# A written-out order replaced by another: loads ahead, no zero matmuls in the head, the last bank read after its last matmul

## The chip, the cores and the metric

The kernel runs on one core of one Trainium2 chip. The metric is the time of one execution on the device in microseconds. Runs before: 199.13, 199.85 and 200.0 us, median 199.85.

## The reference

Attention with a local window and a few global keys, then a two-matrix network with a squared ReLU:

```python
batch, n_heads, seq, head_dim = (4, 8, 768, 64)
n_global, n_local = (8, 96)
...
scores = scale * np.matmul(q, k.transpose(0, 1, 3, 2))
...
keep = is_global | is_local
...
scores = np.where(keep, scores + bias, -1000000000.0)   # bias = -slope of the head * distance
a = softmax(scores);  x = np.matmul(a, v)               # x: 3072 tokens x 512
h = x @ w_in                                            # 512 x 2048
r = np.maximum(h, 0.0)
g = r * r
return (g @ w_out).astype(np.float32)                   # 2048 x 512
```

(The lines of the mask and the softmax are drawn together.) Inputs and output are float32.

## The kernel before, in words

The 3072 tokens are 24 tiles of 128 rows, 6 to each batch element; two tiles make a block, 12 in all. Tile j goes through these steps, which the kernel registers one by one (`plan.op`) under short names:

- `ld` / `load`: POOL starts DMAs that bring q, k and v of the tile to SBUF as bf16 (L304 to L312, issued at L307 for the first loads and at L310 later). Tile 0 is an exception: its q and k come in float32 by SP's queue (L319) into `plain`.
- `tr` (L502): TensorE transposes q (`tr.0.j`) or k (`tr.1.j`) into a PSUM bank, `T` copies the bank to `qkT` on DVE or ACT (L517). From tile 8 on one DMA transpose on SP's queue does both (L536).
- `bias` (tiles 0 to 2, L572) and `sc` (L590): score matmuls into banks, this tile's keys and the tile's before. `gk`, `gv` (L723, L795) copy the eight global keys and values into the neighbour tile; `gv` runs on POOL, DVE or ACT.
- `exp` (L661, on ACT), `mul` (L683, times the exponentiated mask, on DVE), `pv` (L739, values), `norm` (L773, reciprocal and product on DVE).
- `trx` and `xT` (L812 to L833): x transposed on TensorE for tiles 0 to 7, by a DMA on SP's queue for the others (L837).

Blocks 0 and 1 multiply plainly by w_in, in 8 steps (`s1`, L1054, with `relu` L1082 and `sq` L1094), block 0 by w_out in 8 steps (`s2`, L1334). Blocks 2 to 11 take their products in seven parts by sums and differences of quarter matrices: `xs` (L909), `h` (L943) with copies `u` (L973), `c` (L991), `q` (L1011) for w_in, `sum` (L1163), `s2` (L1206), `part` (L1248) and `o` (L1280) for w_out; `isum` and `wsum` prepare the weights. `st` stores the output on SP's queue (L1306).

What sets the order: nothing is scheduled when the kernel is built. `ORDER` (L57) is a string of step names in the order in which the steps are emitted; `Plan.run` (L39) walks through it. A word such as `bias.0.0:23` is step bias of tile 0 in PSUM banks 2 and 3, `T.1.0@V` is step T on DVE (`@A` ACT, `@P` POOL), `s1.0.3#2` is the second step of that name. Each engine runs its own instructions in the order of the string and waits on semaphores for what it reads and for the buffer that it writes; POOL and SP are queues of their own in the same way. The `deps`, `key` and costs that the steps are registered with do not act on a given order.

In the head, after eight warm-up matmuls on a zeroed tile (L371), the string has the transpose of q of tile 0, then the step `warm`: eight more matmuls on zeros (L530, `NKEEP`), then the transpose of k of tile 0. In the last block the half bank of part `p3` is filled in two cuts, of 192 and 64 columns (L1201); the string ends

```
... s2.11.p3.0 s2.11.p3.1
s2.11.p3.0#2 o.11.p3 s2.11.p3.1#2 st.11.0#2 o.11.p3#2 st.11.0#3
```

so the first cut is read by DVE (`o.11.p3`) between the two halves of the second cut.

The loads' order of registration (L414) is not their order of issue; that is in the string too. Its first words issue win.3.0 (a piece of w_in), k of tile 1, q of tile 1, v of tile 0, and loads stay mixed with the work, with `gv.2@P`, `gv.3@P` and `gv.4@P` between them on POOL.

Of the kernel before, what the change touches and what calls it, by code (L numbers as in the profile page):

```python
# [67 lines left out]
pv.4.0:2 ld.wout.1 sq.0.2@V sc.5.0:4157 ld.wout.0 s1.0.4:6 relu.1.2@A exp.5.1.1 s1.0.1:3 sq.1.3@A exp.5.0.0 relu.0.4@V
s1.1.4:7 ld.wout.2 norm.4.0 pv.4.1:4 gv.4@P norm.4.1 sq.0.4@A load.7 exp.5.1.0 sq.1.2@A relu.1.4@A s1.0.0:6 gate.9
ld.wout.4 mul.5.0 s1.0.0#2 sq.1.4@A s1.0.0#3 s1.1.5:2 trx.4:1 exp.5.0.1 relu.1.6@V s1.1.1:4 ld.wout.5 s1.0.1#2  # L70
relu.1.1@A E0.1 mul.5.1 relu.1.5@A pv.5.0:7 s1.1.7:0 s1.1.0:5 sq.1.1@V norm.5.0 ld.wout.6 E0.0 sq.1.5@V tr.1.6:4
sq.1.6@A pv.5.1:2 relu.1.7@A tr.0.6:7 s1.0.0#4 norm.5.1 xT.4@A sq.1.7@A h.2.0.p2:0 ld.wout.7 T.1.6@V h.2.1.p2:1
trx.5:2 xT.5@V relu.1.0@A sq.1.0@A gate.14 h.2.0.p1:5 xs.2.0 s1.0.5:4 sum.1.2 s1.0.7:2 relu.0.1@A xs.2.1 gate.10
sum.1.0 sum.1.1 relu.0.0@A T.0.6@A sc.6.0:36 wsum.0.0 sum.1.3 sq.0.0@A sq.0.1@A s2.0.0.0:7 relu.0.7@A s2.0.1.0 load.9
exp.6.0.0 xs.2.2 s2.0.2.0 exp.6.1.0 s2.0.3.0 s2.0.0.1:2 s2.0.1.1 wsum.2.0 relu.0.5@A sq.0.7@A s2.0.2.1 load.8 mul.6.0
wsum.1.0 s2.0.3.1 tr.0.7:3 tr.1.7:6 gate.15 isum.0.0 h.2.1.p1:4 T.0.7@A s2.0.4.0 isum.0.1 s2.1.p1.0:3 isum.3.1 T.1.7@A
sq.0.5@A pv.6.0:6 isum.1.1 s2.0.4.1 s2.0.5.1 u.2.0.1@A c.2.0.c11 s2.0.5.0 gate.11 u.2.1.1@A h.2.1.p6 q.2.0.c11@A
isum.1.0 T.8 s2.0.6.1 u.2.1.2@A s2.0.6.0 isum.3.0 pv.6.1:0 h.2.0.p6 wsum.2.1 wsum.0.1 s2.1.p1.1 s2.0.7.1 c.2.1.c11
norm.6.0 gate.13 o.0.1@V st.0.1 s2.0.7.0 h.2.1.p7 part.1.p1@A s2.1.p6.0 u.2.0.2@A o.0.0@A u.2.1.3@A h.2.0.p7 h.2.1.p4
T.9 norm.6.1 wsum.3.0 u.2.0.3@A sc.7.0:1762 c.2.1.c21@A wsum.1.1 h.2.1.p5:0 c.2.1.c22 q.2.1.c11@A s2.1.p2.0:4  # L80
exp.7.1.0 exp.7.0.0 isum.2.1 load.10 h.2.0.p4 exp.7.0.1 mul.7.0 exp.7.1.1 s2.1.p2.1 isum.2.0 s2.2.p1.0:7 q.2.1.c21@A
mul.7.1 h.2.0.p5:1 s2.1.p6.1 part.1.p6@A trx.6:6 gate.12 c.2.0.c21@A load.12 pv.7.0:2 xT.6@A c.2.0.c22 q.2.1.c22@A
q.2.0.c22@A s2.2.p1.1 h.2.1.p3 s2.1.p7.0 wsum.3.1 o.1.p2 norm.7.0 h.2.0.p3 pv.7.1:5 s2.1.p7.1 q.2.0.c21@A st.0.0
c.2.1.c12 s2.1.p5.0 s2.1.p5.1 part.1.p7@A q.2.1.c12@A s2.1.p4.0 T.10 s2.1.p4.1 c.2.0.c12 gk.7@V q.2.0.c12@A o.1.p5
o.1.p4@A sc.8.0:6201 st.1.1 part.2.p1@A s2.1.p3.0 norm.7.1 sum.2.0 sum.2.1 s2.1.p3.1 trx.7:5 xT.7@V o.1.p3 h.3.0.p1:3
exp.8.1.0 gk.8@V h.3.1.p1:2 exp.8.0.0 exp.8.1.1 exp.8.0.1 h.3.0.p2:6 xs.3.0 u.3.1.1@A sc.9.0:1540 s2.2.p6.0 mul.8.0
xs.3.1 mul.8.1 u.3.0.1@A h.3.0.p6 exp.9.0.1 exp.9.1.1 gv.7@V h.3.1.p2:4 c.3.0.c11 h.3.1.p6 c.3.1.c11 exp.9.0.0
pv.8.0:0 s2.2.p6.1 pv.8.1:6 load.11 norm.8.0 u.3.1.2@A s2.2.p2.0:1 sum.2.2 gv.8@P q.3.1.c11@A norm.8.1 xT.8 h.3.1.p7
h.3.0.p5:4 u.3.0.2@A h.3.0.p7 s2.2.p2.1 exp.9.1.0 st.1.0 part.2.p6@A xs.3.2 u.3.1.3@A q.3.0.c11@A h.3.1.p5:0 s2.2.p7.0
u.3.0.3@A mul.9.1 mul.9.0 s2.2.p7.1 c.3.1.c22 T.12 c.3.0.c22 pv.9.0:6 h.3.1.p3 o.2.p2 h.3.0.p4 c.3.1.c12 load.15  # L90
norm.9.0 q.3.1.c22@A h.3.0.p3 s2.3.p1.0:5 s2.3.p1.1 c.3.0.c12 q.3.0.c22@A pv.9.1:0 c.3.0.c21@A part.2.p7@A norm.9.1
q.3.1.c12@A h.3.1.p4 q.3.0.c12@A h.4.0.p1:3 c.3.1.c21@A s2.2.p5.0 part.3.p1@A gk.9@V sc.10.0:6402 s2.2.p5.1
q.3.0.c21@A sum.3.0 sum.3.1 s2.2.p4.0 s2.2.p4.1 exp.10.1.0 sum.2.3 exp.10.0.0 exp.10.0.1 h.4.0.p2:4 T.11 u.4.0.1@A
exp.10.1.1 gk.10@V gv.9@A s2.3.p6.0 o.2.p5 mul.10.0 c.4.0.c11 xT.9 h.4.1.p1:6 o.2.p4@A mul.10.1 s2.2.p3.0 s2.2.p3.1
q.3.1.c21@A s2.3.p2.0:0 sum.3.2 u.4.1.1@A pv.10.0:2 pv.10.1:4 s2.3.p6.1 xs.4.0 gate.17 o.2.p3 part.3.p6@A xs.4.1
s2.3.p2.1 norm.10.0 h.4.0.p6 h.4.1.p6 q.4.0.c11@A gv.10@A norm.10.1 u.4.0.2@A load.13 s2.3.p7.0 sc.11.0:7124 u.4.1.2@A
sum.3.3 h.4.0.p7 h.4.1.p7 xs.4.2 exp.11.1.0 o.3.p2 exp.11.0.0 u.4.0.3@V s2.3.p7.1 sc.12.0:17 exp.11.1.1 exp.11.0.1
gate.16 xT.10 h.4.0.p4 c.4.0.c21@A mul.11.0 st.2.0 mul.11.1 h.4.1.p2:4 c.4.1.c11 exp.12.1.0 s2.3.p5.0 pv.11.0:2
pv.11.1:3 s2.3.p5.1 norm.11.0 part.3.p7@A h.4.0.p5:7 q.4.1.c11@A u.4.1.3@A norm.11.1 h.4.1.p5:4 q.4.0.c21@A gate.20
s2.3.p4.0 c.4.0.c22 load.14 s2.3.p4.1 h.4.0.p3 T.13 gate.18 load.16 c.4.1.c22 exp.12.0.0 h.4.1.p4 q.4.1.c22@A h.4.1.p3  # L100
xT.11 s2.4.p2.0:2 h.5.0.p1:3 q.4.0.c22@A o.3.p5 mul.12.0 c.4.0.c12 o.3.p4@A c.4.1.c21@A u.5.0.1@A c.4.1.c12 T.15
s2.3.p3.0 q.4.0.c12@A s2.3.p3.1 q.4.1.c12@V q.4.1.c21@A h.5.0.p2:1 o.3.p3 sc.13.0:5764 st.3.1 st.2.1 h.5.1.p1:0
exp.13.0.0 T.14 s2.4.p2.1 c.5.0.c11 exp.13.1.0 pv.12.1:1 q.5.0.c11@A s2.4.p1.0:5 xs.5.0 sum.4.0 pv.12.0:7 xs.5.1
s2.4.p1.1 mul.13.0 h.5.0.p6 gk.13@V u.5.1.1@A exp.13.0.1 h.5.1.p6 exp.13.1.1 h.5.0.p5:6 sum.4.1 norm.12.0 norm.12.1
h.5.1.p2:4 xs.5.2 mul.13.1 c.5.1.c11 h.5.1.p5:7 u.5.1.2@A sum.4.2 gate.19 part.4.p1@A h.5.1.p7 u.5.0.2@A h.5.0.p7
o.4.p2 u.5.0.3@A c.5.0.c22 pv.13.0:1 u.5.1.3@A norm.13.0 s2.4.p6.0 s2.4.p6.1 xT.12 st.3.0 q.5.1.c11@A T.16 part.4.p6@A
h.5.0.p4 pv.13.1:4 s2.4.p5.0 sum.4.3 c.5.0.c21@A h.5.0.p3 h.5.1.p4 q.5.0.c22@A s2.4.p7.0 norm.13.1 s2.4.p7.1 s2.4.p5.1
c.5.0.c12 q.5.0.c21@A kl.15@V part.4.p7@A c.5.1.c22 q.5.0.c12@A sc.14.0:1346 o.4.p5 s2.4.p4.0 xT.13 exp.14.0.1 kl.14@V
h.5.1.p3 gv.13@P q.5.1.c22@V c.5.1.c12 c.5.1.c21@A s2.4.p4.1 load.17 h.6.0.p1:4 s2.4.p3.0 s2.4.p3.1 exp.14.1.1
exp.14.1.0 exp.14.0.0 sc.15.0:0673 mul.14.1 mul.14.0 xs.6.0 o.4.p4@A xs.6.1 h.6.0.p2:1 o.4.p3 q.5.1.c12@A s2.5.p1.0:5  # L110
u.6.0.1@A c.6.0.c11 exp.15.0.0 exp.15.1.0 exp.15.1.1 sum.5.0 s2.5.p1.1 h.6.0.p6 u.6.0.2@A exp.15.0.1 sum.5.1 load.18
h.6.0.p5:2 part.5.p1@A pv.14.0:0 norm.14.0 pv.14.1:6 h.6.1.p1:1 u.6.1.1@A h.6.0.p7 gv.14@P st.4.0 s2.5.p6.0 u.6.0.3@A
# [1319 lines left out]
```

## Time and profile before

| | |
|---|---|
| runs, median (lowest to highest) | 199.85 us (199.13 to 200.0) |
| profiled execution: its time | 199.37 us |
| its span on the core | 197.6 us |
| granted TensorE clock | 1.00 |
| HBM read / written | 27.26 MB / 6.29 MB |
| output DMAs of 256 KB, issue to landing | 2.5 us |

The span is the time from the first instruction to the last; the execution's own time has 1.8 us around it. PE is TensorE's matmuls, PEld its weight loads, DVE VectorE, ACT ScalarE, POOL GpSimd, SP SyncE; SPq is the queue of DMAs that SP issues. Busy times are unions of the spans of instructions, and neighbours on one engine overlap by some 0.1 us, so that a queue of instructions moves faster than the sum of their durations. A line of the waits reads: engine, what it was to write, its line, then for what it waited: us in total, times, longest. A line of the chain reads: start, length, what held the end at that time. L numbers are lines of the kernel before.

### The profile page before, as it was taken

How to read it: one execution, taken by the hardware profiler on the slowest of the kernel's cores; microseconds unless marked ns; L12 is line 12 of the kernel's file. 1: busy time of each engine (PE TensorE's matmuls, PEld its weight loads, DVE VectorE, ACT ScalarE, POOL GpSimd, SP SyncE). 2: the span in 40 equal slices, each digit the busy share in tenths (PEclk: the TensorE clock that was granted, in tenths of full speed). 3: DMA queues.
4: the chain of work that ended last, by engine and by line, in shares of the span. 5: the costliest groups of instructions: out<-in, count | busy, mean ns of one | idle time of the engine just before them, and what ended most of it. 6: DMA issues, size and time to landing. Idle time of an engine off the chain costs nothing.

```text
span 197.6 us, 6777 instructions
## 1 busy us (share of the span) xinstructions
PE 191.9 (97%) x2776; PEld 169.6 (86%) x2776; DVE 173.2 (88%) x423; ACT 163.0 (82%) x335; POOL 80.4 (41%) x101
## 2 busy tenths in 40 slices
...
PEclk9999999999999999999999999999999999999999
...
GB/s 127 153 158 171 181 181 185 182 202 159 139 209 191 75 200 88 145 174 210 151 129 203 114 124 194 160 121 92 136 81 116 154 55 56 27 30 163 0 106 106
DMA packets 111857, 26.91 MB, mean 136 GB/s; under 512 B 103379, under 2 KB 109011, under 8 KB 111827
## 3 DMA queue, kind: packets, MB, share of 16 engines
...
HBM read 27.26 MB, written 6.29 MB: 170 GB/s over the span
## 4 chain that ended last, share of the span: by engine, by line
PE 95%; DVE 2%; issue 1%; ACT 0%; DVEq 0%
PE bank L1212 35%; PE bank L950 32%; PE bank L1061 7%; PE bank L599 6%; PE bank L748 5%; PE bank L1339 4%; PE bank L372 2%; PE bank L506 2%; PE bank L532 1%; DVE qkT L433 1%; PE bank L816 1%; PE bank L579 0%; ACT qkT L429 0%; DVE o L1287 0%; DVE v L433 0%
## 5 line engine op out<-in xcount | busy, mean ns | idle before, releaser
L1015 ACT ACTIVATE hs<-hr 128x512 bf16<-128x512 f32 x72 | 44.8, 641 | 5.1 <-DVE hr L995 4.7
L665 ACT ACTIVATE esc<-bank 128x512 bf16<-128x512 f32 x78 | 42.9, 614 | 1.3 <-PE bank L599 1.0
L1212 PE MATMUL bank<-wsum,hsum 128*128 128x256 bf16 x264 | 36.2, 273 | 0.0
L1212 PEld LDWEIGHTS <-hsum 128*128 128x128 bf16 x360 | 32.1, 98 | 4.1 <-issue 0.5
L995 DVE CUSTOM_DVE_ANT_0 hr<-bank,early 128x512 f32<-128x512 f32 x45 | 30.4, 685 | 2.5 <-PE bank L950 1.5
L950 PEld LDWEIGHTS <-win 128*128 128x128 bf16 x480 | 29.7, 98 | 1.0
L950 PEld LDWEIGHTS <-qk_first 128*128 128x128 bf16 x480 | 29.7, 98 | 1.0
L429 ACT COPY early<-bank 128x512 f32<-128x512 f32 x42 | 24.5, 591 | 3.6 <-PE bank L950 3.3
L690 DVE TENSOR_TENSOR at<-esc,E 128x1024 bf16<-128x1024 bf16 x39 | 26.7, 696 | 0.1
L1212 PEld LDWEIGHTS <-hs 128*128 128x128 bf16 x264 | 24.0, 98 | 2.6
L310 POOL DMA_DIRECT2D qk<-in_q_dram x18 | 16.0, 890 | 21.9 <-DMA qkT<-qk 20.6
L1212 PE MATMUL bank<-wout,hs 128*128 128x256 bf16 x176 | 24.9, 273 | 0.0
L310 POOL DMA_DIRECT2D v<-in_v_dram x18 | 16.0, 888 | 18.3 <-DVE v L480 14.9
L950 PE MATMUL bank<-xT,win 128*128 128x128 bf16 x320 | 23.4, 219 | 0.0
L431 POOL COPY v<-v 8x520 bf16<-8x520 bf16 x8 | 5.7, 718 | 43.3 <-PE bank L748 43.3
L950 PE MATMUL bank<-xs,qk_first 128*128 128x128 bf16 x320 | 22.8, 219 | 0.0
L779 DVE TENSOR_TENSOR x<-bank,rs 128x256 bf16<-128x256 f32 x48 | 20.4, 425 | 1.7
L865 ACT ACTIVATE hr<-bank 128x512 f32<-128x512 f32 x33 | 19.4, 598 | 1.3 <-PE bank L950 0.4
L748 PE MATMUL bank<-v,at 128*128 128x65 bf16 x352 | 17.8, 193 | 0.0
L1287 DVE TENSOR_TENSOR o<-bank,part 128x256 f32<-128x256 f32 (+2 forms) x34 | 13.8, 410 | 3.3 <-PE bank L1212 3.2
L429 ACT COPY part<-bank 128x256 f32<-128x256 f32 x29 | 10.9, 375 | 7.1 <-PE bank L1212 6.9
L310 POOL DMA_DIRECT2D qk<-in_k_dram x18 | 16.1, 897 | 0.9 <-DMA win<-in_moe_w_in_dram 0.5
...
## 6 DMA issues: line engine op xcount, KB each, us to landing
out_dram<-o SPq DMA_DIRECT2D x22, 256.0 KB, 2.5
v<-in_v_dram POOLq DMA_DIRECT2D x24, 128.0 KB, 5.6
qk<-in_q_dram POOLq DMA_DIRECT2D x18, 128.0 KB, 5.0
qk<-in_k_dram POOLq DMA_DIRECT2D x18, 128.0 KB, 5.8
wout<-in_moe_w_out_dram POOLq DMA_DIRECT2D x8, 256.0 KB, 8.5
win<-in_moe_w_in_dram POOLq DMA_DIRECT2D x6, 256.0 KB, 6.9
qk_first<-in_k_dram POOLq DMA_DIRECT2D x5, 128.0 KB, 5.6
qk_first<-in_q_dram POOLq DMA_DIRECT2D x5, 128.0 KB, 5.7
```

Source lines behind the costliest of these rows:

```text
L310: nc.gpsimd.dma_start(out=dst, in_=src)
L429: nc.scalar.copy(dst, src)
L665: nc.scalar.activation(out=tiles[tag, j, g][:, odd], in_=tiles.pop(("sc", j, odd, g)).rearrange("p a c -> p (a c)"), func=Act.Exp, scale=s ...
L690: nc.vector.tensor_mul(at, tiles.pop(("esc", j, g)), bias)
L748: nc.tensor.matmul(out=po[:, hi, :], lhsT=tiles["at", j, g][:, odd, at * P : (at + 1) * P], rhs=v_sb[kj][:, h, :], start=(i == 0), stop=(i ...
L779: nc.vector.tensor_tensor(out=x[:, 4 * hf : 4 * hf + 4, :], in0=po[:, :, :D], in1=rs.to_broadcast([P, 4, D]), op=Alu.mult,)
L865: nc.scalar.activation(dst, src, Act.Relu)
L950: nc.tensor.matmul(out=tiles["h", blk, g, bank][:, n], lhsT=left_[:, s, k], rhs=right_[:, k], start=opens and n == 0 and k == 0, stop=k == ...
L995: nc.vector._custom_dve(TENSOR_ADD_SAT, out=hr, in0=src, in1=tiles.pop(("u", blk, g, i)), s0=float("inf"), s1=0.0,)
L1015: nc.scalar.activation(hs, hr, Act.Square)
L1061: nc.tensor.matmul(out=hT[:, c, cols], lhsT=w_in_sb[s][:, kt, c * P : (c + 1) * P], rhs=tiles["xT", blk][:, kt, cols], start=(kt == 0), st ...
L1212: nc.tensor.matmul(out=tiles["acc", blk, bank][:, cols], lhsT=left_[:, s], rhs=right_[:, cols], start=first and s == 0, stop=s == NSTEP - ...
```

## The change

The whole string is replaced. Its first lines, before and after:

```diff
-tr.0.0:0 warm:7 tr.1.0:1 T.1.0@V bias.0.0:23 T.0.0@A sc.0.0 ld.win.3.0 exp.0.0.0 ld.k.1 tr.1.1:4 bias.1.0:5670 T.1.1@V ld.q.1
-tr.0.1:1 ld.v.0 exp.0.1.0 T.0.1@V sc.1.0 exp.1.0.1 pv.0.0:2 ld.q.2 tr.0.2:3 norm.0.0 ld.k.2 T.0.2@V ld.k.3 exp.1.1.1
-pv.0.1:4 tr.1.2:1 bias.2.0:7203 ld.v.1 norm.0.1 exp.1.1.0 ld.q.3 tr.1.3:6 gk.1@A T.1.2@A sc.2.0 exp.1.0.0 T.1.3@V
-ld.k.4 pv.1.0:4 ld.v.2 gk.2@V exp.2.1.0 exp.2.1.1 norm.1.0 trx.0:1 xT.0@A ones.6 pv.1.1:5 tr.0.3:6 T.0.3@V exp.2.0.0
-tr.1.4:2 ld.win.6.0 sc.3.0:4361 ld.q.4 norm.1.1 ld.v.3 trx.1:7 gv.1@V exp.2.0.1 exp.3.0.0 pv.2.0:5 exp.3.1.0 exp.3.0.1
-T.1.4@V xT.1@V pv.2.1:0 ld.k.5 ld.win.2.0 exp.3.1.1 gk.3@A ld.win.2.1 norm.2.0 s1.0.3:2 mul.3.0 s1.0.6:4 ld.win.4.0
-tr.0.4:7 ld.q.5 ld.v.4 norm.2.1 mul.3.1 relu.0.6@A s1.0.3#2 gv.2@P pv.3.0:3 norm.3.0 trx.2:5 T.0.4@A pv.3.1:6
-ld.win.1.0 norm.3.1 ld.win.0.1 xT.2@A sc.4.0:1047 exp.4.1.1 exp.4.1.0 tr.1.5:3 T.1.5@A s1.0.2:5 trx.3:6 xT.3@V
...
+ld.q.1 ld.k.1 ld.v.0 ld.q.2 ld.k.2 ld.k.3 ld.v.1 ld.q.3 ld.q.5 ld.v.2 ld.k.4 ld.q.4 ld.k.5 ld.v.3 ld.win.6.0
+ld.win.3.0 ld.win.2.0 ld.v.4 ld.win.0.0 ld.win.0.1 ld.win.2.1 ld.v.5 ld.win.1.0 ones.6 load.6 ld.win.5.0 ld.wout.0
+ld.win.4.0 ld.wout.1 ld.wout.2 ld.win.7.0 ld.wout.3 load.7 ld.wout.4 ld.wout.5 ld.wout.6 ld.wout.7 tr.0.0:0 T.0.0@V
+gate.9 tr.1.0:1 T.1.0@A tr.0.1:2 bias.0.0:34 sc.0.0 exp.0.0.0 T.0.1@A tr.1.1:5 T.1.1@V bias.1.0:6701 exp.0.1.0 sc.1.0
+pv.0.1:3 tr.0.2:5 exp.1.0.1 exp.1.1.1 pv.0.0:2 norm.0.0 norm.0.1 tr.1.2:4 exp.1.0.0 gk.1@V T.0.2@V T.1.2@V tr.1.3:0
+bias.2.0:1263 pv.1.1:5 T.1.3@A exp.1.1.0 pv.1.0:4 gv.1@V sc.2.0 exp.2.1.0 norm.1.0 tr.0.3:0 T.0.3@V exp.2.1.1 tr.0.5:7
+trx.0:4 gk.2@V exp.2.0.1 exp.2.0.0 sc.3.0:2036 exp.3.1.1 exp.3.0.1 xT.0@V norm.1.1 mul.3.1 exp.3.1.0 pv.2.1:4 pv.2.0:5
+exp.3.0.0 trx.1:1 tr.1.4:6 T.1.4@A T.0.5@A norm.2.0 tr.0.4:3 gv.2@V tr.1.5:0 xT.1@A T.0.4@V gk.3@V mul.3.0 T.1.5@A
+sc.4.0:2563 pv.3.1:7 pv.3.0:1 norm.2.1 trx.2:0 gk.4@V exp.4.0.1 exp.4.1.0 exp.4.0.0 norm.3.0 sc.5.0:4651 norm.3.1
+mul.4.0 gv.3@A trx.3:2 s1.0.6:7 xT.2@V exp.4.1.1 mul.4.1 exp.5.0.0 exp.5.1.0 s1.0.3:3 s1.0.3#2 E0.1 xT.3@V pv.4.0:0
...
```

All the first loads stand ahead, and in the string q of tile 1 comes ahead of its k. Later on, loads and SP's transposes stand in groups: `load.9 load.8 T.8 T.9`, then `load.10 load.11 load.12`, then `T.10 T.11 load.14`, and so on. The end of the string:

```diff
-s2.11.p5.1 o.11.p5 st.11.1 st.11.0 sum.11.3#2 s2.11.p4.0 s2.11.p4.1 o.11.p4@A st.11.1#2 s2.11.p3.0 s2.11.p3.1
-s2.11.p3.0#2 o.11.p3 s2.11.p3.1#2 st.11.0#2 o.11.p3#2 st.11.0#3
+s2.11.p4.0 s2.11.p4.1 o.11.p4@A o.10.p3 st.10.0 o.11.p5 st.11.1 st.11.1#2 s2.11.p3.0 s2.11.p3.1 s2.11.p3.0#2
+s2.11.p3.1#2 o.11.p3 st.11.0#2 o.11.p3#2 st.11.0#3
```

The step `warm` is gone:

```diff
-    NKEEP = 8
...
-        if j == 0:
-            def emit_warm(e):
-                for _ in range(NKEEP):
-                    nc.tensor.matmul(out=psum(), lhsT=zero[:, :P], rhs=zero, start=True, stop=True)
-
-            plan.op(("warm",), {"PE": 0.216 * NKEEP}, emit_warm, key=base)
```

The buffers of the copies `u` are taken from a list of free ones instead of in turn:

```diff
-    u_next = [0]
+    u_free = list(u_ring)
...
-                    u = u_ring[u_next[0] % NU]
-                    u_next[0] += 1
+                    u = u_free.pop(0)
...
+                        u = tiles.pop(("u", blk, g, i))
+                        nc.vector._custom_dve(TENSOR_ADD_SAT, out=hr, in0=src, in1=u, s0=float("inf"), s1=0.0)
+                        u_free.append(u)
```

The other edits change what the steps are registered with, and no instruction in the given order: `pv` names the load of the tile before among its dependences, `o.11.p3` of both cuts names the last matmuls of the bank, and `open_sc` / `emit_sc` count their banks through (`at`).

Built, the program has 5524 PE rows instead of 5540 (a weight load and a matmul for each of the eight zeros), 425 DVE rows instead of 408, and the same number on SP.

More of the change, by code (lines that the diff above doesn't have):

```diff
@@ L68 @@
[L68 to L112, printed above, removed]
@@ new lines @@
+q.3.1.c22@A s2.2.p6.0 s2.2.p6.1 h.3.1.p3 gk.9@A c.3.1.c21@A q.3.1.c11@A c.3.1.c12 s2.2.p2.0:6 s2.2.p2.1 h.3.0.p4
+part.2.p6@A c.3.0.c22 pv.9.1:7 s2.2.p7.0 gv.9@P load.13 load.15 s2.2.p7.1 q.3.1.c21@A norm.9.0 norm.9.1 c.3.0.c21@A
+q.3.1.c12@A gate.17 q.3.0.c22@V o.2.p2 sc.10.0:2531 h.4.0.p1:7 sum.2.3 h.3.0.p3 s2.2.p5.0 exp.10.1.0 s2.2.p5.1
+part.2.p7@A s2.2.p4.0 exp.10.0.0 exp.10.0.1 s2.2.p4.1 mul.10.0 o.2.p5 xT.9 T.13 exp.10.1.1 s2.2.p3.0 u.4.0.1@A
+s2.2.p3.1 c.3.0.c12 q.3.0.c12@A mul.10.1 pv.10.0:5 o.2.p3 st.2.0 st.1.1 pv.10.1:2 norm.10.0 norm.10.1 xs.4.0 gv.10@P
```

159 lines of the change are left out of this document (98 added, 61 removed).

## The prediction

> **What bounds the kernel now.** I read the page first, then what TensorE (PE) waited for, then wide windows.
>
> ```profile
> span 197.6 us, 6777 instructions
> PE 191.9 (97%) x2776; PEld 169.6 (86%) x2776; DVE 173.2 (88%) x423; ACT 163.0 (82%) x335; POOL 80.4 (41%) x101
> PEclk9999999999999999999999999999999999999999
> PE 95%; DVE 2%; issue 1%; ACT 0%; DVEq 0%
> ```
> ```profile
> PE bank L372 <- DVE early L361: 1.2, 1, 1.2
> PE bank L599 <- DVE qkT L433: 1.1, 3, 0.5
> PE bank L1212 <- DVE o L1287: 0.5, 1, 0.5
> ```
> ```profile
> 20.00:60.00 40.00, 40.00 (x534) 33.30 (x531) 36.76 (x87) 35.06 (x70) 26.49 (x34) 1.00 1.72 179
> 60.00:100.00 40.00, 40.00 (x638) 37.05 (x637) 37.27 (x92) 35.92 (x74) 15.65 (x19) 1.00 1.55 155
> 100.00:140.00 40.00, 40.00 (x635) 36.57 (x633) 38.23 (x91) 37.38 (x79) 15.84 (x19) 1.00 1.45 145
> ```
>
> PE carries 95% of the chain that ended last, and the three lines are all that it waited for: 1.2 us before its first matmul, three waits in the head, one in the last block. From 20 us on it is busy without a hole (the columns of the windows are PE, weight loads, DVE, ACT, POOL, clock, DMA). No row has PE waiting for a DMA. So between 21 us and the last block a reordering has nothing to take away; it can only add holes. What can change is the head, the tail, and how close DVE comes to its limit: 38.23 of 40 us in one stage already.
>
> **The change part by part.** The sum is made against the profiled execution, 199.37 us with a span of 197.6; the median of the three runs is 199.85, so 0.48 above it.
>
> *1. The zeros.* The chain in order of time, the weight loads, and the two loads that matter:
>
> ```profile
> 1.19 3.60 PE bank L372 x8
> 4.79 0.85 PE bank L506 x4
> 5.64 2.41 PE bank L532 x8
> 8.05 0.45 PE bank L506 x4
> 9.28 0.40 PE bank L599 x8
> 10.00 0.87 PE bank L579 x8
> 19.61 0.22 PE bank L506 x4
> 21.11 0.55 PE bank L599 x16
> ```
> ```profile
> 6.71 0.15 PEld L532 LDWEIGHTS <-early 128*128 128x128 bf16 x1 [0.28 <-issue]
> 7.03 0.53 PEld L532 LDWEIGHTS <-early 128*128 128x128 bf16 x3 [0.16 <-issue]
> 7.67 0.57 PEld L506 LDWEIGHTS bank<-ident,plain 128*128 128x128 f32 x4
> ```
> ```profile
> 1.25 0.56 SPq L319 DMA_DIRECT2D plain<-in_k_dram  x1
> 1.34 0.89 POOL L307 DMA_DIRECT2D win<-in_moe_w_in_dram  x1 [0.17 <-issue]
> DMA to landing us min/median/max: 3.1/4.6/6.0
> ```
>
> The eight zero matmuls (L532) take 2.41 us. Taking them out does not give 2.41 us, since behind them stands the transpose of k of tile 0, and that k, issued at 1.25, took the longest time to land, 6.0 us: 7.25. The transpose began at 7.67. What is late next is that landing: 0.4 us are there to gain.
>
> The landing itself may move. In the trace SP's queue had moved all but a few packets of k by 5 us:
>
> ```profile
> q1 hardware_dynamic: 94, 0.02, 12.4%
> q1 hardware_dynamic: 16, 0.00, 2.6%
> ```
>
> (its packets in the windows 4 to 5 and 6 to 7 us). The stragglers crept at 16 a microsecond beside POOL's first load, a w_in piece of long rows. After the change POOL's first load is q of tile 1, of short rows. Bounds: k lands at 5.0, the end of the bulk, or at 7.25 as before; I take 6.2, in the middle.
>
> What the zeros also did is to keep PE running. The first matmuls (8 in 3.60 us, 0.45 each) run at half the rate of the last zeros (three weight loads in 0.53 us from 7.03 on, so some 0.21 apart; the loads at 6.71 and 7.03 still stand 0.32 apart); likewise the four fp32 transposes take 0.85 us at 4.79 and 0.45 at 8.05. The full rate came at about 6.9 us, after 5.7 us without a hole, though the granted clock reads full throughout. Without the zeros PE has a hole from 5.64 to about 6.25. Bounds: the full rate comes at 6.9 all the same (0 us), or only after 5.7 fresh us of work, at about 12 (some 2.5 us, all that is queued until then taking twice its time). I take the middle, half rate to about 10. Then from the start of k's transpose (6.25): 1.3 us to its last weight load and drain (0.85 + 0.45 of issue, against 0.9 now), the transpose of q of tile 1 0.44, eight bias matmuls 0.87, scores 0.6: the first exp can start at 6.25 + 3.2 + 0.05 = 9.5, against 9.71 now (at full rate it stands 9.71 - 7.67 = 2.0 us behind the start of k's transpose). The next bias (16 half-tiles of work, 0.87) is half slow: 0.4 more before the scores of tile 1.
>
> [...]
>
> *2. The head's order.* The new order brings the scores of tiles 4 and 5 ahead of the first w_in matmuls (L1061). Compare at a point of equal PE work: now at the start of the scores of tile 4 (21.11), PE has done, beyond what both share, w_in steps 3 and 6 of block 0; at the end of the transpose of x of tile 3, the new order has done instead the scores of tiles 4 and 5, two transposes of tile 5 and that one.
>
> ```profile
> 32.65 1.75 PE bank L1061 x16
> 9.71 1.09 ACT L665 ACTIVATE at<-bank 128x512 bf16<-128x512 f32 x2 [3.44 <-PE bank L599]
> 17.31 2.12 ACT L665 ACTIVATE esc<-bank 128x512 bf16<-128x512 f32 x4
> 13.81 0.61 ACT L429 COPY qkT<-bank 128x512 bf16<-128x512 bf16 x1
> 19.95 0.68 DVE L690 TENSOR_TENSOR at<-esc,E 128x1024 bf16<-128x1024 bf16 x1
> 20.56 0.18 DVE L778 RECIPROCAL rs<-bank 128x4 f32<-128x4 f32 x1
> 21.15 0.18 DVE L778 RECIPROCAL rs<-bank 128x4 f32<-128x4 f32 x1
> ```
>
> That is 8 x 0.11 twice, 1.75 us, against 2 x 0.55 + 3 x 0.22 = 1.76: equal. Now PE gets there 21.11 - 9.71 = 11.4 us after the first exp. In the new order, counted from the first exp (exps 0.48 apart, 0.61 for the last; an ACT copy 0.6 when waited for; a DVE product 0.61, from 19.95 to the next start; a norm 0.59, from the two reciprocals): exp and copy of q of tile 1 1.06, scores of tile 1 to 1.85; three exps, a copy and the fourth exp to 4.36; last values product and scores of tile 2 to 5.15; its four exps to 7.2; scores of tile 3 lie in between, its third exp ends at about 8.4. Here DVE has the turn: product, norm of tile 2, copies of v and of q of tile 4, the global k: the scores of tile 4 can start at 10.4. Then product, norm, global k, and the two norms of tile 3 to 12.7, and the transpose to 13.0. So 13.0 against 11.4: **+1.6 us**, with PE idle because the w_in matmuls that now fill this time are queued behind. Bounds: 11.4 (DVE's turn hidden, no loss) to 13.8 (a few more gaps of 0.1 to 0.2).
>
> *3. Loads.* POOL issues one load each 0.89 us (its load at 1.34, above):
>
> ```profile
> qk_first<-in_q_dram POOLq DMA_DIRECT2D x5, 128.0 KB, 5.7
> win<-in_moe_w_in_dram POOLq DMA_DIRECT2D x6, 256.0 KB, 6.9
> qkT<-qk SPq DMA_TRANSPOSE x16, 3.8
> ```
>
> Moved past the copies of v on POOL, the first 26 loads go without a stop: k of tile 5 (13th) lands at 1.34 + 12 x 0.89 + 5.7 = 17.7, the first w_in piece (15th) at 1.34 + 14 x 0.89 + 6.9 = 20.7, both ahead of use (by part 2, about 9.5 + 8.5 and 22.5). k of tile 6 (26th), 1.34 + 25 x 0.89 + 5.7 = 29.3, or a little more, is just in time for its transpose at 31: nothing, at worst 1 us. Keeping the SP transposes of q and k apart from the loads gains nothing I can find: they land in 3.8 us and PE never waited for one; on SP's queue, where stores and the transposes of x wait behind them, they stand 4 us of PE work or more ahead of use. [...]
>
> *4. The last bank.*
>
> ```profile
> 193.18 0.94 PE L1212 MATMUL bank<-wout,hsum 128*128 128x192 bf16 x12
> 194.16 0.36 DVE L1287 TENSOR_TENSOR o<-bank,part 128x192 f32<-128x192 f32 x1 [0.84 <-PE bank L1212]
> 194.57 0.28 PE L1212 MATMUL bank<-wout,hsum 128*128 128x64 bf16 x4 [0.45 <-DVE o L1287]
> 194.88 0.22 DVE L1287 TENSOR_TENSOR o<-bank,part 128x64 f32<-128x64 f32 x1 [0.37 <-PE bank L1212]
> ```
>
> Now the last four matmuls wait for the read of 192 columns. After, they follow at once (0.28 less some 0.17 of drain: 0.11), the reads start at 194.27 and the last ends at about 194.77 instead of 195.10: **-0.3 us**. Bounds -0.45 to 0.
>
> *5. Between.* Built, the new order has 17 more DVE and 14 fewer ACT instructions (copies, squares and sums moved), at 173.2/423 = 0.41 us each **7 us** more DVE; counted along the order, 5 of them ahead of block 5's first product, at about 90 us. Spread over the first two windows they make 36.76 and 37.27 of 40 into some 39 and 40. Where DVE is late, banks are not free and PE waits. Below 38.23 it did not. Bounds 0 to +2; I take +0.4.
>
> The sum: first exp -0.2, slow bias +0.4, head +1.6, tail -0.3, DVE +0.4: +1.9, so 201.3 beside the profiled execution and 201.75 beside the median. I forecast **201.5**.
>
> **Rivals.**
> - *The clock is at full rate by 6.9* (for: the hole is short; against: it took 5.7 us without a hole). The first exp then is at 6.25 + 2.0 = 8.2: -1.5 + 1.6 - 0.3 + 0.4 = +0.2, so 199.8, no change.
> - *The head's DVE turn is hidden as well*, the side on which the kernel is faster: it decides whether the scores of tile 4 come at 10.4 or at about 9 after the first exp. Then -1.5 + 0 - 0.3: 197.8. Against: the order on DVE is fixed, and its product waits for an exp at 8.4.
> - *k lands no sooner than now* and the clock is slow: the first exp at 7.3 + 3.25 = 10.5, +0.8 instead of -0.2: 202.5. For: nothing in the change touches that load.
> - *DVE becomes the bound* between 30 and 90 us and PE waits 2 us instead of 0.4: 203.1. For: part 5's 39 and 40 of 40. Against: busy spans overlap, so 40 is not yet full.
> - *The order does not do what it says*: a load is held by its buffer, not by its place, so loads and transposes still overlap. No time of its own, as part 3 costs it at nothing.
>
> **How the numbers follow.** The forecast 0.35; full clock 0.20; hidden turn 0.10; late k 0.20; DVE the bound 0.15. The range leaves out the hidden turn and the top of DVE, 0.2 at most, and reaches from the full clock with a head 1 us shorter to a late k with most of DVE's 2 us: 198.8 to 203.8. A measurement of this kernel tells about 0.5% from no change. Faster by more: the hidden turn and a little of the full clock, 0.14. Within: most of the full clock and the forecast's low end, 0.24. Slower: 0.62.
>
> **What would show it.** Right: no L532; a hole on PE from 5.6 to the transpose of k, weight loads at half rate after it; PE waiting in the head between 15 and 23 us for DVE and ACT; first L1061 at 22 to 23 us, not 18.3; no PE wait between the last two reads. Wrong: a first exp before 9 us, PE dense from 17 us, or waits of PE on DMAs, which I cost at nothing.

## The result, and the profile after

The changed kernel takes 201.97 us (median of 4 runs, 201.53 to 202.33) against 199.62 us (4 runs, 199.13 to 200.0): a ratio of 1.0122 (95% interval 1.0094 to 1.015), 2.35 us more. The profiled execution took 202.32 us with a span of 200.6, 3.0 us more span than the profiled execution before. Ratios, here and further on, leave out the few executions in a slower state; medians count every run.

Its page: span, busy time, granted clock by slice, and the chain that ended last.

```profile
span 200.6 us, 6757 instructions
PE 193.0 (96%) x2768; PEld 169.7 (85%) x2768; DVE 180.1 (90%) x439; ACT 157.4 (78%) x320; POOL 79.5 (40%) x100
PEclk9998899999999999999999999999999999999998
PE 57%; DVE 17%; DMA 13%; POOL 8%; issue 2%; ACT 0%; DVEq 0%; POOLq 0%
```

The eight zeros are gone, some 2 us of work, and yet PE is busy 1.1 us more. DVE has the 7 us that were forecast (180.1 against 173.2), and the clock, full in every slice before, dips near 20 us. Before, PE carried 95% of the chain; now DVE, DMA and POOL hold parts of it. In order of time it runs over POOL's loads and their landings, with some DVE work, to 51 us, over DVE to 60.7 us, and mostly over PE from there; DVE carries it again from 134 to 150 and from 187 to 192 us. Some of its pieces:

```profile
14.36 7.03 DMA win<-in_moe_w_in_dram
...
25.03 7.54 DMA wout<-in_moe_w_out_dram
32.86 7.02 DMA qk<-in_k_dram
...
46.31 4.76 DMA v<-in_v_dram
...
58.02 0.69 DVE hr L990
60.69 0.60 PE bank L1206 x4
```

So a lead of PE in the head need not last: loads and DVE are close behind it. The head of the kernel on PE, with the first exp on ACT:

```profile
4.58 1.38 PE L506 MATMUL bank<-ident,plain 128*128 128x128 f32 x8
16.62 0.40 PE L506 MATMUL bank<-ident,qk_first 128*128 128x128 bf16 x4 [0.40 <-DMA qk_first<-in_k_dram]
18.11 0.23 PE L594 MATMUL bank<-qkT 64*128 64x128 bf16 x2 [1.09 <-DVE qkT L433]
22.23 1.93 PE L1055 MATMUL bank<-xT,win 128*128 128x256 bf16 x24
```
```profile
7.32 0.60 ACT L660 ACTIVATE at<-bank 128x512 bf16<-128x512 f32 x1 [0.74 <-PE bank L594]
```

k is transposed directly behind q, and the first exp starts at 7.32 us, not 9.71. From there PE loses it again: it waits 0.44 us for k of tile 3 (at 10.35 us) and 0.40 for k of tile 5, then 1.09 us for a DVE copy ahead of the scores of tile 4, and comes to its first w_in matmul at 22.23 (before: 18.12, with the scores of tiles 4 and 5 still to do). Three windows of the head (PE, weight loads, DVE, ACT, POOL, then the granted clock):

```profile
16.00:18.00 2.00, 0.62 (x8) 0.37 (x6) 1.97 (x6) 2.00 (x5) 2.00 (x3) 1.00 1.51 166
18.00:19.00 1.00, 0.82 (x16) 0.69 (x15) 0.97 (x5) 0.72 (x2) 1.00 (x3) 0.74 1.34 177
19.00:21.50 2.50, 2.36 (x35) 1.70 (x32) 1.62 (x5) 2.17 (x5) 1.74 (x3) 0.50 1.92 172
```

After 2 us in which PE was busy for 0.62, the granted clock is 0.50, and the scores of tiles 4 and 5 run at half rate (from 18.56 us on their pairs of matmuls start 0.106 us apart; at 8.5 us, with the clock full, 0.056). Then the middle:

```profile
60.00:100.00 40.00, 39.92 (x627) 36.22 (x624) 38.39 (x94) 35.44 (x77) 18.05 (x22) 1.00 1.74 165
100.00:140.00 40.00, 40.00 (x627) 36.46 (x623) 38.38 (x92) 36.34 (x75) 14.24 (x17) 1.00 1.56 150
```

PE looks full, but these counts cover short holes: a group's busy time runs to the modelled end of its last matmul (one of 256 columns is recorded as 0.273 us long, and the next starts 0.109 behind it; of 128 columns 0.219 and 0.056). The starts show the holes, on PE and then on DVE:

```profile
59.56 1.06 PE L945 MATMUL bank<-xT,win 128*128 128x128 bf16 x16
60.69 0.60 PE L1206 MATMUL bank<-wsum,hs 128*128 128x256 bf16 x4
...
149.45 0.60 PE L1206 MATMUL bank<-wsum,hs 128*128 128x256 bf16 x4
150.34 0.61 PE L945 MATMUL bank<-xT,win 128*128 128x128 bf16 x8 [0.29 <-DVE x L774]
```
```profile
60.22 0.42 DVE L433 COPY part<-bank 128x256 f32<-128x256 f32 x1
...
149.87 0.42 DVE L774 TENSOR_TENSOR x<-bank,rs 128x256 bf16<-128x256 f32 x1
```

Sixteen matmuls of 128 columns stream in 16 x 0.056 = 0.89 us at these distances, so the next could start at 60.45; it starts at 60.69, 0.05 after a DVE copy out of a bank ends. Four of 256 columns stream in 4 x 0.109 = 0.44, so 149.89; the next starts at 150.34, again as a DVE read of a bank ends. There are five such holes between 58 and 150 us (0.27, 0.24, 0.16, 0.15, 0.45: 1.27 us). Four end with a DVE instruction; the first, at 58.77, ends with a read on DVE and one on ACT that finish 0.01 us apart. Before, there is none over 0.12 us between 21 us and the last block.

To compare kernels whose orders differ, I sum at each moment the streaming time of the matmuls still to come (0.056, 0.11, 0.22 us for 128, 256, 512 columns, the distance at which their starts stand in these traces), and compare the times at which the same amount is left. Against the profiled execution before, after is 1.15 us late at 53 us, 1.8 at 64, 2.7 at 174 and still at 189, 2.8 at 192 and 3.0 at the end. So about a third of the loss is the head; more is the middle; the last block loses 0.2, and the end wins nothing.

### The profile page after: what moved, and what is told of

It reads as the page before. It is cut to its first block, busy times and chain, and to the rows that moved or that the text cites. A ratio compares the mean times of both kernels' runs of the same rounds, so it can differ in the third digit from the quotient of the medians.

```text
span 200.6 us, 6757 instructions
## 1 busy us (share of the span) xinstructions
PE 193.0 (96%) x2768; PEld 169.7 (85%) x2768; DVE 180.1 (90%) x439; ACT 157.4 (78%) x320; POOL 79.5 (40%) x100
## 4 chain that ended last, share of the span: by engine, by line
PE 57%; DVE 17%; DMA 13%; POOL 8%; issue 2%; ACT 0%; DVEq 0%; POOLq 0%
PE bank L1206 26%; PE bank L945 25%; POOL qk_first L307 4%; DMA wout<-in_moe_w_out_dram 4%; DVE hr L990 4%; DMA win<-in_moe_w_in_dram 4%; DMA qk<-in_k_dram 4%; PE bank L743 3%; PE bank L594 3%; DMA v<-in_v_dram 2%; DVE at L685 2%; DVE hsum L1161 2%; DVE wsum L1126 2%; POOL v L307 2%; DVE x L774 1%
## 5 line engine op out<-in xcount | busy, mean ns | idle before, releaser
L1009 ACT ACTIVATE hs<-hr 128x512 bf16<-128x512 f32 x70 | 43.0, 635 | 6.7 <-DVE hr L990 6.1
L660 ACT ACTIVATE esc<-bank 128x512 bf16<-128x512 f32 x78 | 41.9, 603 | 2.7 <-PE bank L594 1.4
L1206 PEld LDWEIGHTS <-hsum 128*128 128x128 bf16 x360 | 32.6, 98 | 3.8 <-DVE hsum L1161 0.3
L1206 PE MATMUL bank<-wsum,hsum 128*128 128x256 bf16 x264 | 35.5, 273 | 0.0
L990 DVE CUSTOM_DVE_ANT_0 hr<-bank,early 128x512 f32<-128x512 f32 x44 | 29.7, 685 | 2.3 <-PE bank L945 1.1
L429 ACT COPY early<-bank 128x512 f32<-128x512 f32 x40 | 23.1, 587 | 8.2 <-PE bank L945 7.9
L860 ACT ACTIVATE hr<-bank 128x512 f32<-128x512 f32 x31 | 18.5, 599 | 8.8 <-PE bank L1055 5.2
L945 PE MATMUL bank<-xs,qk_first 128*128 128x128 bf16 x320 | 23.3, 219 | 0.0
L743 PE MATMUL bank<-v,at 128*128 128x65 bf16 x352 | 17.7, 196 | 0.0
L743 PEld LDWEIGHTS <-at 128*128 128x128 bf16 x352 | 15.1, 99 | 1.7 <-issue 0.2
L431 POOL COPY v<-v 8x520 bf16<-8x520 bf16 x7 | 4.4, 627 | 30.1 <-PE bank L743 30.1
```

What stands on the lines that cost most here:

```text
L429: nc.scalar.copy(dst, src)
L660: nc.scalar.activation(out=tiles[tag, j, g][:, odd], in_=tiles.pop(("sc", j, odd, g)).rearrange("p a c -> p (a c)"), func=Act.Exp, scale=s ...
L743: nc.tensor.matmul(out=po[:, hi, :], lhsT=tiles["at", j, g][:, odd, at * P : (at + 1) * P], rhs=v_sb[kj][:, h, :], start=(i == 0), stop=(i ...
L860: nc.scalar.activation(dst, src, Act.Relu)
L945: nc.tensor.matmul(out=tiles["h", blk, g, bank][:, n], lhsT=left_[:, s, k], rhs=right_[:, k], start=opens and n == 0 and k == 0, stop=k == ...
L990: nc.vector._custom_dve(TENSOR_ADD_SAT, out=hr, in0=src, in1=u, s0=float("inf"), s1=0.0)
```

## The experiments

Each is a median beside runs of before on the same chip, and the ratio with its 95% interval.

| kernel | us | before | ratio |
|---|---|---|---|
| before_tail_only | 199.49 | 199.60 | 0.9994 (0.9972 to 1.0016) |
| before_without_zeros | 200.02 | 199.60 | 1.0016 (0.9990 to 1.0041) |
| before_no_zeros_win3_later_tail | 199.78 | 199.60 | 1.0024 (0.9998 to 1.0051) |
| after_with_zeros | 203.80 | 199.60 | 1.0205 (1.0156 to 1.0253) |
| before_head_after_rest | 201.85 | 199.55 | 1.0109 (1.0083 to 1.0135) |
| lean_head_after_rest | 201.96 | 199.55 | 1.0121 (1.0087 to 1.0156) |
| after_head_before_rest | 204.04 | 199.55 | 1.0212 (1.0180 to 1.0244) |
| after_copies_as_before | 227.35 | 199.55 | 1.1377 (1.1337 to 1.1416) |
| lean_loads_ahead_of_copy | 201.00 | 199.40 | 1.0079 (1.0052 to 1.0105) |
| after_q4_copy_first | 202.29 | 199.40 | 1.0143 (1.0116 to 1.0170) |
| after_two_copies_on_act | 202.07 | 199.40 | 1.0149 (1.0122 to 1.0175) |
| after_q4_and_global_k_first | 202.59 | 199.80 | 1.0141 (1.0106 to 1.0176) |

### The last read alone (before_tail_only)

```diff
-s2.11.p3.0#2 o.11.p3 s2.11.p3.1#2
+s2.11.p3.0#2 s2.11.p3.1#2 o.11.p3
```

> Kernel before, with one word of the order moved: the read of the first 192 columns of the last bank stands behind the last matmul. Theory (the prediction's part 4): the last matmuls follow at once and the end comes 0.3 us sooner (0 to 0.45), ratio about 0.9985. Rival: the reads on VectorE, not the matmuls, set the end, so nothing is gained (0).

The timed runs can't tell 0.3 us from nothing: the interval holds both. The trace shows no gain, for a reason that neither theory named. The last reads on DVE of this kernel, and the last store on SP of this kernel and of before:

```profile
194.96 0.49 DVE L1282 TENSOR_TENSOR o<-bank,part 128x192 f32<-128x192 f32 x2 [0.96 <-PE bank L1207]
```
```profile
195.76 0.38 SPq L1304 DMA_DIRECT2D out_dram<-o  x1
```
```profile
195.13 0.33 SPq L1309 DMA_DIRECT2D out_dram<-o  x1
```

This execution is 0.68 us behind before's from 106 us on (below). Without that, the reads end at 195.45 - 0.68 = 194.77 instead of 195.10, the 0.33 us that were forecast; but both stores are now issued at the end, 0.42 us apart on SP, so the last is issued at 195.08 instead of 195.13. In before, the first store went out while PE and DVE did the last columns. One wait took the other's place.

The 0.68 us are a wait of DVE for a transpose of x on SP's queue:

```profile
105.66 0.42 DVE L917 TENSOR_TENSOR xs<-xT 128x512 bf16<-128x512 bf16 x1 [0.72 <-DMA xT<-x]
```

The same product started at 104.77 in before's profiled execution, without a wait. So before has this wait in some executions, and that profile showed one that escaped it.

### The zeros: away from before, back into after

```diff
-tr.0.0:0 warm:7 tr.1.0:1
+tr.0.0:0 tr.1.0:1
```

> Kernel before without the 8 matmuls of zeros and nothing else: win step 3 is still the first load of the POOL queue. Theory A (the load order decides when k lands): k still lands at about 7.25 us, so that at most 0.4 us of PE's time is won, first exp at 9.3 with the clock at full rate: 0 to -0.4 us. Theory B (the hole on PE keeps it at half rate): weight loads of the transposes at 0.21 us and more apart after the hole, first exp at about 10.5, +0.8 us. Theory C (the zeros themselves hold up k's transpose): first exp near 7.3 as in the changed kernel, -2.4 us.

The second kernel also has the load moved, and the last read as above:

```diff
-ld.win.3.0 exp.0.0.0
+exp.0.0.0
...
-ld.k.4 pv.1.0:4
+ld.k.4 ld.win.3.0 pv.1.0:4
```

> Kernel before without the zeros, with the load of win step 3 moved from the first place of the POOL queue behind k of tile 4, and with the last read as in after; the head's order, copies and everything between stay those of before. Theory A (k lands early because POOL's first load has short rows, and the new head order and the middle cost time): k lands at about 5.2, first exp at 7.3, gain 1.5 to 2.4 from there and 0.3 at the end: 197 to 198, faster than both kernels. Rival 1 (loads of the next tiles become the bound once the first exp is early): gain 0.5, 199. Rival 2 (win step 3 comes late for its matmuls at 18 us, +1 us or more): 199 to 200.5.

Without zeros alone, PE and then DVE:

```profile
4.58 1.91 PE L500 MATMUL bank<-ident,plain 128*128 128x128 f32 x8
7.28 0.40 PE L587 MATMUL bank<-qkT 64*128 64x128 bf16 x8 [0.27 <-DVE qkT L427]
17.82 1.05 PE L1049 MATMUL bank<-xT,win 128*128 128x256 bf16 x8 [1.12 <-DMA win<-in_moe_w_in_dram]
```
```profile
105.17 0.43 DVE L910 TENSOR_TENSOR xs<-xT 128x512 bf16<-128x512 bf16 x1 [0.99 <-DMA xT<-x]
```

Theory C holds at the start: k is there as soon as q is transposed, and the first scores come at 7.28 instead of 9.28, with win step 3 still the first load of POOL. So the load order does not decide when k lands. Over the 14 traces of this study k lands in 3.9 to 4.4 us in all but one, and the one with 6.0 is the execution from which I predicted. But the 2.0 us go: PE waits 1.12 us for win step 6, which had landed when PE was later, and what is left (0.7 us, by the starts of the same matmuls) goes at 105 us, where DVE waits 0.99 us for the transpose of x; behind it this execution is 0.2 us later than before's. With the load moved, PE is 2.2 us ahead at the first scores and 1.15 at the scores of tile 4 (19.89 against 21.04), and in the profiled execution 0.74 at 190 us. But that execution (198.67 us) is the fastest of its twelve; the timed runs show no gain on average, and theory A's 197 to 198 did not come. Without the zeros before's order is not faster.

```diff
-tr.0.0:0 T.0.0@V gate.9 tr.1.0:1
+tr.0.0:0 warm:7 T.0.0@V gate.9 tr.1.0:1
```

> Kernel after, with the 8 matmuls of zeros put back between the transposes of q and k. In it k lands at 5.25 us. Theory A (both steps are needed): the zeros hold PE until about 7 us, so the first exp goes from 7.3 to about 9.3 and the head's end moves by as much as VectorE's and ScalarE's turn does not absorb: +1.0 to +2.0 us against after, 203 to 204. Rival: the head is bound by loads that land later (k of tiles 2 and 5), so the later first exp is absorbed: within 0.5 us of after, 202.

(this one against after, with the step `warm` written in again)

The first exp goes to 9.75, 2.4 us later, and the time to 203.8, as theory A has it. By the ratios (1.0205 against 1.0122) the zeros cost some 1.7 us in after's order, though the intervals nearly touch; in before's order leaving them out wins nothing.

### Halves of the order

The order of one kernel up to a seam, the rest in the order of the other, banks renumbered at the seam. At the seam of the first, against before (the second has the same seam, and the edits of the lean head ahead of it):

```diff
 exp.7.1.1 s2.1.p2.1 isum.2.0
-s2.2.p1.0:7 q.2.1.c21@A mul.7.1 h.2.0.p5:1 s2.1.p6.1
+gate.12 load.11 load.12 st.0.0 T.10 T.11 load.14 trx.6:7
```

> The order of before up to about 57 us (zeros, loads, transposes, all of block 0 and 1), and from there the order of after with its engines, transposes and loads, banks renumbered at the seam. Theory (after loses 1.1 us in the head and some 1.3 us in holes of the middle that VectorE leaves, and wins 0.3 at the end): before + 1.3 - 0.3, 200.6. Rival 1 (all of the loss is the head): 199.3. Rival 2 (the new middle keeps loads off the transposes of x, and so takes away a wait that before has at its VectorE product xs in most executions, 0.7 us at 105 us in two of the traces): 199.0 to 199.5, with no wait for a DMA after 57 us.

> As the kernel of before's head and after's rest, but without the zeros and with the load of win step 3 behind k of tile 4. Theory (a lead won in the head is kept if no load and no transpose takes it back): the lead over before at 57 us is 0.7 to 1.0 us as in the trace of the kernel that had the same head, so 0.7 to 1.0 us less than the run with before's head, 198.5 to 199.9. Rival (whatever the head wins is given back at a later wait, as it was in that kernel): the same time as the run with before's head, within 0.3 us.

The third, against after:

```diff
 c.2.0.c22 q.2.0.c22@A q.2.0.c11@A
-s2.1.p5.0 pv.7.0:3 norm.7.0 q.2.1.c21@A
+sum.1.3 wsum.3.0 s2.2.p1.0:5 q.2.1.c21@A
```

> The order of after up to about 54 us (no zeros, all loads first, scores of tiles 4 and 5 ahead of the w_in matmuls), and from there the order of before with its engines and its last read. Theory (the head costs 1.1 us and the rest its share of the loss): 199.6 + 1.1 = 200.7, with the same wait at xs around 106 us as before in some executions. Rival (the loss is in the middle and the tail): 199.6.

With before's head, after's rest costs 2.3 us (1.0109), more than the theory had. By the work left, 0.95 of it are lost by 64 us, and 1.3 come later, with holes of the same size in the same places as after: 0.16 at 91.6, 0.15 at 136.1, 0.45 at 149.1, 0.22 at 191.2. These belong to the order of the rest. The 0.95 do not all: PE passes the seam at 52.9 us, and 0.77 are holes at 53.1 (0.22) and 54.2 us (0.55), which after does not have there:

```profile
54.77 0.60 PE L1207 MATMUL bank<-wsum,hsum 128*128 128x256 bf16 x4 [0.39 <-DVE o L1282]
```

They may be the cut's own. So the rest costs between 1.5 and 2.3 us; after's own order loses 1.75 to 1.95 from 53 us on (below). No DVE product waits for a transpose of x, here as in after. The lean head gains nothing (201.96 against 201.85). The third kernel has a hole of its own at the seam:

```profile
57.22 0.61 PE L1199 MATMUL bank<-wout,hs 128*128 128x256 bf16 x4 [2.28 <-ACT hs L1002]
```

That is an artefact of the cut, so 204.04 says little about the head. Less 2.3, it would be 201.7, some 2.2 us over before, of which 0.6 are again a hole ahead of `xs`, at 109.6. Of the five traces with before's rest, beside before's own, four show that DVE wait at 0.4 to 1.0 us, and one (below) at 2.2; of the eight with after's rest none shows it over 0.2.

### The engines of the middle

```diff
-part.6.p1@V
+part.6.p1@A
...
-gv.9@P
+gv.9@A
```

(two of 53 words)

> Kernel after, with its order, but behind 57 us every copy, square and sum on the engine that it has in before (53 of them change engine, 9 more on ScalarE than in after). Theory (VectorE near its limit leaves the holes of the middle): -0.5 to -1.3 us against after, 200.7 to 201.5. Rival (the order itself leaves them, or ScalarE becomes late for the copies that it gets back at places that were not made for it): 202 or more.

227 us answers neither. The waits of PE in it begin with

```profile
PE bank L737 <- POOL v L425: 10.3, 2, 8.7
```

and POOL, ahead of the longest of them, does this:

```profile
110.95 0.88 POOL L304 DMA_DIRECT2D qk<-in_q_dram  x1 [5.73 <-DMA qkT<-qk]
...
115.28 0.62 POOL L425 COPY v<-v 8x520 bf16<-8x520 bf16 x1
```

Among the 53 are copies of v that before has on POOL. In after's order such a copy stands behind loads that wait for a transpose of q or k, and PE waits for the copy. Which engine does a copy and where it stands are one decision. A narrower trial:

```diff
-gk.16@V
+gk.16@A
...
-part.1.p7@V
+part.1.p7@A
```

> Kernel after, with two copies on ScalarE as in before, those that VectorE does just ahead of two of the holes on PE: the copy of the global k of tile 16 (at 148.9 us in after, hole of 0.45 us at 149.8) and the copy of a partial sum of block 1 (at 60.2 us, hole of 0.24 at 60.4). Theory (VectorE is late there because it got those copies): both holes go, -0.4 to -0.7 us, 201.3 to 201.6. Rival (VectorE or ScalarE is late at the next bank instead): the holes move or grow, 202 or more.

I had named the wrong copy: that of tile 16 is at 111.4 us, and the one ahead of the hole at 149.8 is of tile 21, and stayed on DVE. So that hole was not tried. The other trial is clear:

```profile
61.05 0.61 PE L939 MATMUL bank<-xs,qk_first 128*128 128x128 bf16 x8
62.01 0.61 PE L939 MATMUL bank<-xs,qk_first 128*128 128x128 bf16 x8 [0.34 <-ACT early L423]
```

The hole at 60.4 is gone, and one of 0.51 us stands 1 us later, where ACT, which now has the copy, is late with its own. The rival holds: at this place neither engine has room, and the time is no better. That DVE's load as such leaves the other holes stays argued, not shown.

This trace is also a second execution of after's head, unchanged. Two of its windows and its first w_in matmul:

```profile
16.00:18.00 2.00, 0.93 (x11) 0.55 (x9) 1.97 (x6) 2.00 (x5) 2.00 (x3) 1.00 1.66 170
...
19.00:21.50 2.50, 2.07 (x41) 1.43 (x40) 2.33 (x7) 2.50 (x5) 2.14 (x4) 1.00 1.93 173
```
```profile
21.43 0.82 PE L1049 MATMUL bank<-xT,win 128*128 128x256 bf16 x6
```

Here the clock stays full, and PE is 0.8 us earlier than in the profiled execution, though the scores of tile 4 start alike (18.09 and 18.11 us): the 0.8 us are lost behind that start, where one runs at the half rate (granted clock 0.50 from 19.0 to 21.5 us, against 1.00). By the work left, this one is 0.3 us behind before's at 53 us, not 1.15, and then loses 1.75 up to 174 us, about as after does (1.55). The two executions with other heads below lose 1.45 and 1.7 there.

### Loads off the transpose in before's order

```diff
-h.5.1.p3 gv.13@P
+h.5.1.p3 load.17 load.18 gv.13@P
```

> The kernel with before's order, without zeros, with the load of win step 3 behind k of tile 4 and the last read as in after, and with the loads of tiles 17 and 18 moved in POOL's order ahead of the copy of v of tile 13, for which POOL waits until 98 us. In that kernel those six loads run from 97.6 to 102.8 us, and the transpose of x issued at 98.8 lands late for VectorE's product at 105 us. Theory (what the lean head wins is lost there, to loads beside a transpose): the loads go out from about 93 us, the wait of PE at 105 us goes, and the total is 0.7 to 1.0 us below before, 198.5 to 198.9. Rival 1 (the loss is elsewhere, or the loads collide with the next transpose just as well): 199.6, no gain. Rival 2 (a buffer holds the loads, and POOL is later for the copy of v): slower, 200 or more.

Worse, by 1.1 us against the same kernel without the move, going by the ratios. POOL, SP and DVE:

```profile
95.67 0.88 POOL L304 DMA_DIRECT2D qk<-in_q_dram  x1 [2.72 <-DMA qkT<-qk]
...
99.13 0.92 POOL L304 DMA_DIRECT2D qk<-in_k_dram  x1
```
```profile
99.01 1.21 SPq L828 DMA_TRANSPOSE xT<-x  x1
```
```profile
106.61 0.42 DVE L910 TENSOR_TENSOR xs<-xT 128x512 bf16<-128x512 bf16 x1 [2.21 <-DMA xT<-x]
```

The buffers hold five of the six loads until 95.67, so that four of these have been issued when the transpose starts; it takes 7.6 us, against 5.4 without the move, where two of the six are ahead of it, and DVE waits 2.2. The time is rival 2's, and buffers do hold the loads; but PE waits there for `xs`, not for the copy of v, so the mechanism is the collision of rival 1. Of the 195 transposes of x whose landing the 14 traces hold, 48 have no load of POOL under way before they land: they take 2.4 to 4.1 us, median 2.5. The 40 with five or more take 3.4 to 7.6, median 5.1. In these traces a transpose with loads beside it lands later, and here that costs PE.

### DVE's turn in the head

```diff
-norm.2.0 tr.0.4:3 gv.2@V tr.1.5:0 xT.1@A T.0.4@V
+tr.0.4:3 T.0.4@V norm.2.0 gv.2@V tr.1.5:0 xT.1@A
```

> Kernel after, with one VectorE copy moved: q of tile 4 is copied out of its bank ahead of the norm of tile 2 and the copy of v of tile 2 instead of behind them; nothing else changes. Theory (VectorE's turn ahead of the scores of tile 4 is what holds PE from 16.8 to 18.1 us in after): the scores of tile 4 start at 17.2 instead of 18.1, and with a shorter hole the granted clock falls less or not at all, so -0.9 to -1.6 us at the first w_in matmul (22.2 us in after) and 200.4 to 201.1 in all. Rival 1 (the landing of k of tile 5, or ScalarE's copies, hold the scores just as long): within 0.3 us of after. Rival 2 (the norm and the copy that are now later hold the next product): the same.

PE waits next for the copy that stands behind:

```profile
17.48 0.36 PE L588 MATMUL bank<-qkT 64*128 64x128 bf16 x2
18.38 0.23 PE L588 MATMUL bank<-qkT,qkT 64*128 64x128 bf16 x2 [0.53 <-DVE qkT L427]
```

The first two matmuls come 0.63 us sooner, the others hardly: they need the global part of k, too. The clock falls here as well, at 19 us, and the first w_in matmul comes at 22.03:

```profile
16.00:17.00 1.00, 0.45 (x5) 0.29 (x6) 1.00 (x3) 1.00 (x3) 1.00 (x2) 1.00 1.83 163
17.00:18.00 1.00, 0.70 (x6) 0.26 (x6) 0.97 (x6) 1.00 (x3) 1.00 (x2) 1.00 1.45 187
...
19.00:20.00 1.00, 1.00 (x19) 1.00 (x18) 0.17 (x1) 1.00 (x3) 1.00 (x3) 0.50 1.75 178
```

So the copy of the global k moves as well:

```diff
-mul.3.1 exp.3.1.0
+gk.3@V mul.3.1 exp.3.1.0
...
-T.0.4@V gk.3@V mul.3.0
+mul.3.0
```

> Kernel after, with the copy of q of tile 4 moved as in the run with that copy alone, and with the copy of the global part of k of tile 3 moved as well, into the 0.86 us in which VectorE waits ahead of the product of tile 3. In the run with the copy alone the first two score matmuls of tile 4 came 0.63 us sooner and the others waited for that second copy until 18.4 us. Theory (VectorE's turn, of both copies, holds the head): all scores of tile 4 start at 17.3 to 17.5, -0.7 us, and -0.7 to -1.5 us at the first w_in matmul (22.2 us in after), the more if the granted clock no longer falls; 200.5 to 201.3 in all. Rival 1 (behind the copies the exps on ScalarE and the landing of loads hold the scores of tile 5 just as long): within 0.3 us of after at 22 us. Rival 2 (the granted clock falls to half for about 3 us all the same and takes back half of it): -0.3 us.

```profile
17.23 0.40 PE L500 MATMUL bank<-ident,qk_first 128*128 128x128 bf16 x4 [0.98 <-DMA qk_first<-in_k_dram]
17.56 0.23 PE L588 MATMUL bank<-qkT 64*128 64x128 bf16 x2
...
20.67 1.93 PE L1049 MATMUL bank<-xT,win 128*128 128x256 bf16 x24
```

In the head the theory holds: the scores of tile 4 wait for DVE no longer (now for k of tile 5), and the first w_in matmul comes at 20.67, 0.8 us before the trace with the same order and a full clock. The profiled execution is the fastest of its six, 201.54; their median is 202.59, no better than after. By the work left the lead over that other trace is 0.1 us at 53. In between, PE has four waits that the other trace has not, 0.7 us together: for DVE at 28.8, 31.7 and 35.7 us, and until 43.5 us for a piece of w_out that lands at 43.46. So the head's lead is paid back to DVE's next turns and to a load; where it goes in the timed runs stays open. No version tried beats before.

## Why the prediction was right or wrong, point by point

The total (201.5, measured 201.97) and the sign were right, through errors that cancel: that is luck. Of the signs that the prediction names, the first w_in matmul at 22.23 us and the waits for DVE ahead of it are there, but so are two of the three that were to show it wrong, a first exp before 9 us and waits of PE on DMAs.

- *The zeros, first exp at 9.5: wrong.* It came at 7.32. Two inputs failed. k's landing at 6.2 (bounds 5.0 to 7.25) came from the one trace of 14 in which it was late; elsewhere it is 5.2 to 5.7. And half rate to about 10 us did not happen: the eight fp32 transposes take 1.38 to 1.91 us over the traces without zeros, and from 6.6 us on, until the clock falls in some of them, all runs at the full rate (eight bias matmuls of 256 columns take 1.04 us at 7.46 us in after, 7.67 and 7.93 in before's order without zeros). That was the rival of a full clock; its 199.8 did not come, since the rest cost more.
- *The head's order, +1.6: right in mechanism, too small as it was counted.* From the first exp, 13.0 us were forecast (bounds 11.4 to 13.8); it took 14.9 us (7.32 to 22.23), and 14.2 with the clock full (7.22 to 21.43). The error, 1.9 and 1.2 us, made up for most of the 2.2 by which the first exp came sooner than forecast. Like for like, without zeros on either side, before's order is at this point at 19.89: +2.3 and +1.5. That DVE holds the scores of tile 4 is shown by the last experiment; that this sets the time further on is not, since the lead won there is gone by 53 us. Not foreseen: the fall of the granted clock to 0.50 behind the hole in some executions.
- *Loads and transposes, nothing: wrong both ways.* PE waited 0.8 us for k of tiles 3 and 5. They landed no later than forecast (k of tile 5 at 16.58, forecast 17.7), but with the earlier first exp PE wanted them sooner. And the new order does take away a wait, that of `xs`, 0 to 1 us in before's order, which the one trace I had did not show.
- *The last bank, -0.3: wrong.* The engines end 0.33 us sooner, and the issue of two stores on SP takes it back.
- *Between, +0.4 (bounds 0 to 2): inside its bounds, but too small, and mostly in another place.* 1.45 to 1.75 us between 53 and 174 us, in four traces, and 0.2 in the last block. The rival in which PE waits 2 us placed them between 30 and 90 us; there after loses 0.4, and the other 1.2 between 90 and 174. DVE's 7 us came as forecast (the traces have 16 more DVE rows and 15 fewer on ACT, not 17 and 14). I read DVE's 38.23 of 40 us as room. It is an average, and in 100 to 140 us DVE is hardly busier than before (38.38): each hole stands where a few DVE instructions lie back to back and PE needs what one of them frees or writes.

Summed again: head +0.3 to +1.1, middle and last block +1.75 to +1.95, end 0, against before's profiled execution; and some 0.7 less where before has its wait at `xs`. The medians are 2.35 apart.
